# Batch 0's transposes one pair ahead, half of its queries and keys by casting DMA, and a new load order on GpSimd

## The chip, the cores and the metric

The kernel runs on one core of a Trainium2 chip. The metric is the device time of one execution in microseconds (us); each version was run several times, and medians are quoted with their range. The profile shown of a version is of one execution under the hardware profiler, for every version but the kernel before one of those counted; its span is some 1.7 us shorter than the time of the same execution. All runs quoted here are of the fast state.

Names: PE is the matrix engine, DVE VectorE, ACT ScalarE, POOL GpSimd, SP the engine that only issues transfers.

## The reference

```python
# q, k, v: (B=8, H=8, S=576, D=64); beacon_k, beacon_v: 16 more keys and values per head, never masked
k_all = concat([beacon_k, k], axis=2); v_all = concat([beacon_v, v], axis=2)
scores = q @ k_all.T / sqrt(D)           # causal mask over the 576 ordinary keys
a = softmax(scores)
x = (a @ v_all)                          # (B*S, H*D) = (4608, 512)
h = max(x @ w1, x @ w2, x @ w3)          # d_ff = 768
out = h @ w_out                          # (4608, 512) float32
```

## The kernel before: the parts that matter

The kernel goes through 32 head pairs, four to a batch. A pair's queries and keys are turned on PE by 28 transposes, copied out of PSUM by DVE, and give scores in six steps; ACT takes the exponentials. Every second pair, the value products of a finished quad of heads are put between the score steps. From batch 1 on, the feed-forward units of the batch before fill PE's gaps. Batch 0 has no such filler. Its first ten feed-forward units come in a block behind batch 0's last value products, and batch 1 starts behind them.

```python
def emit_transposes(p):                       # pair p of batch b
    ...
    if b == 0:                                # batch 0 arrives in float32 and is cast on the engines
        q32, k32 = stage.pop(pi)
        nc.vector.tensor_copy(q_sb[:, pair_heads(pi), :], q32)
        nc.scalar.copy(k_sb[:, pair_heads(pi), :], k32)
    q_ps = turn(qs, QP, QR)                   # 12 transposes on PE
    k_ps = turn(ks, KP, KR)                   # 16 transposes on PE
    for e in range(2):
        nc.vector.tensor_copy(qz[p % NQZ][e][hs], q_ps[hs])
    nc.vector.tensor_copy(kT, k_ps.rearrange("d r p -> d p r"))
...
def emit_all():
    load_qk_first(0); load_qk_first(1)        # float32, queues of SP and ACT
    for t in range(n_kt): build_mask(t)       # POOL
    for t in range(n_kt): load_v(0, t)        # casting DMA, POOL's queue, as all below
    load_w_in(0, d_ff // 2); load_w_in(d_ff // 2, d_ff)
    load_w_out()
    load_qk(1, slice(0, H))
    for t in range(n_kt): load_v(1, t)
    emit_transposes(0)
    for p in range(NPAIR):
        for c in range(len(chunks)):          # six score steps
            emit_scores(p, c)                 # 2 matmuls, 2 exponentials, masks
            if p != PPB and p >= 2 and p % 2 == 0 and 1 <= c <= 3:
                emit_pv(p // 2 - 1, c - 1)    # value products
            if c == 3 and p + 1 < NPAIR and p + 1 != PPB:
                if b == 0 and pi < 2: load_qk_first(pi + 2)
                emit_transposes(p + 1)
            ...
        if p == PPB - 1:                      # end of batch 0
            ... # last value products, ten feed-forward units
            emit_transposes(p + 1)            # first pair of batch 1
```

The softmax here doesn't subtract the row's maximum and nothing guards it: scores larger than these inputs give would overflow.

## Time and profile before

| | before |
|---|---|
| median of 3 runs | 345.58 us (345.57 to 346.87) |
| profiled span | 343.9 us |
| PE busy, whole span | 91% |
| first exponential of batch 0 | 9.75 us |
| first feed-forward matmul | 41.54 us |
| from there to the end | 302.3 us |

The prediction shows the views that matter: the slices of the span, the instructions in order of time, and the stages of batch 0. In the timeline the first two numbers are start and length in us, and the bracket is how long the engine had stood idle and what ended it. In a stage line the numbers behind the stretch and its length are busy us and instruction counts of PE, PE's weight loads, DVE, ACT and POOL, then the granted clock of PE, the share of the DMA engines (the times of all packets over those of 16 engines, so it can pass 1) and GB/s.

I call the time up to the first feed-forward matmul the ramp, and the rest the stretch. In the stretch PE is nearly full.

### The profile page before, as it was taken

How to read it: one execution, taken by the hardware profiler on the slowest of the kernel's cores; microseconds unless marked ns; L12 is line 12 of the kernel's file. 1: busy time of each engine (PE TensorE's matmuls, PEld its weight loads, DVE VectorE, ACT ScalarE, POOL GpSimd, SP SyncE). 2: the span in 40 equal slices, each digit the busy share in tenths (PEclk: the TensorE clock that was granted, in tenths of full speed). 3: DMA queues.
4: the chain of work that ended last, by engine and by line, in shares of the span. 5: the costliest groups of instructions: out<-in, count | busy, mean ns of one | idle time of the engine just before them, and what ended most of it. 6: DMA issues, size and time to landing. Idle time of an engine off the chain costs nothing.

```text
span 343.9 us, 9797 instructions
## 1 busy us (share of the span) xinstructions
PE 311.6 (91%) x4011; PEld 174.4 (51%) x4064; DVE 185.8 (54%) x338; ACT 187.0 (54%) x507; POOL 162.0 (47%) x441
## 2 busy tenths in 40 slices
PE   1676897989999999999999999999999999999993
PEld 1344543545565556565655555555555555444441
DVE  4445354456565655655565556565555564545552
ACT  2675626875666557665757475647573765120210
POOL 6778105982666367636753575457542433000000
PEclk9998799999999999999999999999999999999999
DMA  8999950991993189306940694059713100402204
GB/s 171 194 188 158 184 38 2 154 60 32 173 108 27 32 137 145 27 22 117 173 26 4 132 172 34 2 105 181 46 8 93 34 2 3 122 2 52 70 2 123
DMA packets 62165, 28.85 MB, mean 84 GB/s; under 512 B 42792, under 2 KB 56920, under 8 KB 62120
## 3 DMA queue, kind: packets, MB, share of 16 engines
q0 software_dynamic: 54880, 16.38, 45.6%
q1 hardware_dynamic: 6928, 11.24, 12.0%
q8 instruction: 32, 0.52, 0.6%
q10 hardware_dynamic: 312, 0.59, 0.6%
q14 instruction: 13, 0.11, 0.1%
HBM read 35.13 MB, written 9.44 MB: 130 GB/s over the span
## 4 chain that ended last, share of the span: by engine, by line
PE 73%; DVE 9%; DMA 8%; POOL 5%; issue 3%; ACT 1%; DVEq 0%
PE fps L332 32%; PE fps L349 12%; PE sc L247 10%; PE pv L293 10%; PE sc L332 5%; DMA k_sb<-in_k_dram 4%; PE sc L208 3%; DVE kT L226 2%; DVE hT L342 2%; DMA v_sb<-in_v_dram 2%; DMA w_sb<-in_moe_w_dram 2%; PE sc L349 2%; POOL w_sb L171 2%; DVE xT L310 1%; POOL at_sb L271 1%
## 5 line engine op out<-in xcount | busy, mean ns | idle before, releaser
L255 ACT ACTIVATE at_sb<-sc 128x288 bf16<-128x288 f32 (+4 forms) x384 | 129.0, 406 | 77.4 <-PE sc L247 74.7
L271 POOL TENSOR_SCALAR_AFFINE_SELECT at_sb<-at_sb 128x57 bf16<-128x57 bf16 (+1 forms) x336 | 93.5, 300 | 113.1 <-ACT at_sb L255 109.0
L332 PE MATMUL fps<-xT,w_sb 128*128 128x512 bf16 x540 | 141.4, 379 | 4.8 <-issue 2.7
L342 DVE TENSOR_TENSOR hT<-hT,fps 128x512 bf16<-128x512 bf16 x96 | 65.8, 686 | 66.0 <-PE fps L332 55.7
L332 PEld LDWEIGHTS <-w_sb 128*128 128x128 bf16 x648 | 59.6, 98 | 58.7 <-issue 3.6
L247 PEld LDWEIGHTS <-kT 128*128 128x128 bf16 (+1 forms) x384 | 38.6, 106 | 46.7 <-DVE kT L226 6.5
L340 ACT CAST hT<-fps 128x512 bf16<-128x512 f32 x48 | 28.2, 587 | 42.8 <-PE fps L332 37.7
L349 PE MATMUL fps<-w_out_sb,hT 128*128 128x512 bf16 x171 | 42.7, 380 | 1.6 <-issue 1.3
L310 DVE TENSOR_TENSOR xT<-pv,recip 128x288 bf16<-128x288 f32 x64 | 27.7, 454 | 29.6 <-ACT recip L305 22.4
L161 POOL DMA_DIRECT2D v_sb<-in_v_dram x40 | 34.0, 860 | 6.1 <-DMA w_out_sb<-in_moe_w_out_dram 3.7
L293 PE MATMUL pv<-at_sb,v_sb 128*32 128x288 bf16 (+4 forms) x1280 | 33.1, 242 | 0.2 <-ACT lnd L303 0.2
L357 DVE COPY y<-fps 128x512 f32<-128x512 f32 x31 | 21.4, 690 | 20.8 <-PE fps L349 16.4
L247 PE MATMUL sc<-qz_107,kT 128*128 128x288 bf16 (+2 forms) x96 | 28.4, 300 | 4.5 <-DVE kT L226 3.6
L293 PEld LDWEIGHTS <-v_sb 128*32 128x32 bf16 (+1 forms) x1280 | 25.8, 98 | 12.6 <-issue 11.3
L247 PE MATMUL sc<-qz_111,kT 128*128 128x288 bf16 (+2 forms) x96 | 28.8, 301 | 2.2 <-DVE kT L226 1.8
L349 PEld LDWEIGHTS <-hT 128*128 128x128 bf16 x216 | 19.5, 98 | 20.0 <-DVE hT L342 0.4
L247 PE MATMUL sc<-qz_113,kT 128*128 128x288 bf16 (+2 forms) x96 | 28.7, 301 | 0.3
L247 PE MATMUL sc<-qz_109,kT 128*128 128x288 bf16 (+2 forms) x96 | 28.4, 302 | 0.2 <-DVE kT L226 0.2
L226 DVE COPY kT<-sc 128x592 bf16<-128x592 bf16 x28 | 21.7, 775 | 0.9
L208 PEld LDWEIGHTS <-q_sb 96*64 96x64 bf16 x384 | 10.7, 114 | 18.9 <-DVE q_sb L219 13.2
L293 PE MATMUL pv<-at_sb,ones 128*32 128x288 bf16 (+4 forms) x640 | 18.7, 246 | 0.6 <-DVE xT L310 0.6
L332 PE MATMUL sc<-xT,w_sb 128*128 128x512 bf16 x71 | 18.4, 379 | 0.1
(50 smaller groups left out, 190.0 us busy)
## 6 DMA issues: line engine op xcount, KB each, us to landing
out_dram<-y SPq DMA_DIRECT2D x24, 192.0 KB, 2.2
q_sb<-in_q_dram POOLq DMA_DIRECT2D x7, 576.0 KB, 7.4
k_sb<-in_k_dram POOLq DMA_DIRECT2D x7, 576.0 KB, 11.2
v_sb<-in_v_dram POOLq DMA_DIRECT2D x24, 128.0 KB, 4.7
out_dram<-y SPq DMA_DIRECT2D x24, 128.0 KB, 2.2
w_sb<-in_moe_w_dram POOLq DMA_DIRECT2D x24, 96.0 KB, 5.5
out_dram<-y SPq DMA_DIRECT2D x24, 64.0 KB, 1.6
v_sb<-in_v_dram POOLq DMA_DIRECT2D x8, 112.0 KB, 4.5
```

What stands on the lines that cost most here:

```text
L161: nc.gpsimd.dma_start(out=v_sb[lo : lo + n, t], in_=v[b, :, t0 : t0 + n, :].rearrange("h p d -> p h d"),)
L226: nc.vector.tensor_copy(kT, k_ps.rearrange("d r p -> d p r"))
L247: nc.tensor.matmul(ps[0:n, 0 : nr * w].rearrange("k (r p) -> k r p", p=w), kT[:, 128 * t : 128 * t + n], qz[p % NQZ][e][:, r0:r1, p0:QP], ...
L255: nc.scalar.activation(out=at_sb[0:n, t, j0 + e, r0:r1, p0:QP], in_=sc[e][0:n, 0 : nr * w].rearrange("k (r p) -> k r p", p=w), func=AF.Exp ...
L271: nc.gpsimd.affine_select(out=view, in_=view, compare_op=ALU.is_ge, fill=0.0, base=QR * p0 + r0 - k_tok[t], pattern=[[1, nr], [QR, p1 - p0 ...
L293: nc.tensor.matmul(ps[32 * j : 32 * j + 32, :, p0:QP], lhsT, at_sb[0:n, t, j, rs, p0:QP], start=(t == 0), stop=(t == n_kt - 1), tile_posit ...
L310: nc.vector.tensor_mul(xs.rearrange("c (r p) -> c r p", p=QP), ps, state["recip", hf])
L332: nc.tensor.matmul(ps, w_in[i][:, ct, 128 * ft : 128 * (ft + 1)], xT[:, ct, t0 : t0 + TOKB], start=(ct == 0), stop=(ct == n_ct - 1),)
L340: nc.scalar.copy(hT[:, ft, :], ps)
L342: nc.vector.tensor_max(hT[:, ft, :], hT[:, ft, :], ps)
L349: nc.tensor.matmul(ps, hT[:, ft, 128 * tt : 128 * (tt + 1)], w_out_sb[:, ft, :], start=(ft == 0), stop=(ft == n_ft - 1),)
L357: nc.vector.tensor_copy(y, ps)
```

## The change

Three things are meant to shorten the ramp. The next pair's transposes are issued behind the pair's first score step, and no longer behind its fourth, so that their copies are ready when the pair ends. Pairs 2 and 3 of batch 0 come in bfloat16 by casting DMA, so that ACT and DVE need not cast them. On POOL's queue pair 2 comes first of all, masks are built between value loads, and batch 1's queries and keys go ahead of the output weight.

```diff
-        if b == 0:                                   # in emit_transposes
-            q32, k32 = stage.pop(pi)
-            nc.vector.tensor_copy(q_sb[:, pair_heads(pi), :], q32)
-            nc.scalar.copy(k_sb[:, pair_heads(pi), :], k32)
+    def cast_first(pi):                              # now its own function, for pairs 0 and 1
+        ...
         load_qk_first(0)
         load_qk_first(1)
-        for t in range(n_kt):
-            build_mask(t)
+        load_qk(0, pair_heads(2))
+        make_identity(nc, ident)                     # was at the head of the kernel
         for t in range(n_kt):
             load_v(0, t)
+            if t == 2:
+                for u in range(n_kt):
+                    build_mask(u)
+        load_qk(0, pair_heads(3))
         load_w_in(0, d_ff // 2)
         load_w_in(d_ff // 2, d_ff)
+        load_qk(1, slice(0, H))
         load_w_out()
-        load_qk(1, slice(0, H))
...
+        cast_first(0)
         emit_transposes(0)
+        cast_first(1)
...
-                emit_scores(p, c)
+                if p < PPB - 1 and c == 0:
+                    emit_scores(p, c, lambda: emit_transposes(p + 1))   # between exponentials and masks
+                else:
+                    emit_scores(p, c)
...
-                if c == 3 and p + 1 < NPAIR and p + 1 != PPB:
-                    if b == 0 and pi < 2:
-                        load_qk_first(pi + 2)
+                if c == 3 and b > 0 and p + 1 < NPAIR:
                     emit_transposes(p + 1)
```

## The prediction

> **The bound.** I first read the page's busy shares: the matrix engine (PE) is busy for 91% of the 343.9 us. The 40 slices show where the other 9% is: from the ninth slice on PE stands at 8 or 9 tenths, but the first five read 1, 6, 7, 6, 8. The ramp, batch 0's attention, is not PE bound, and the change touches only that.
>
> ```profile
> PE   1676897989999999999999999999999999999993
> DMA  8999950991993189306940694059713100402204
> ```
>
> Each digit is 8.6 us. DMA is at 8 or 9 for the first five slices, then alternates: the start is also when everything is loaded.
>
> Next the instructions in order of time (start, length, engine, line, work, idle before), from the middle of head pair 0 to the first scores of pair 1:
>
> ```profile
> 12.08 0.30 DVE L267 TENSOR_TENSOR at_sb<-at_sb,mask 128x264 bf16<-128x264 bf16 x1 [0.75 <-ACT at_sb L255]
> 12.47 1.08 ACT L220 CAST k_sb<-k_125 74x1024 bf16<-74x1024 f32 x1
> 12.76 0.30 DVE L267 TENSOR_TENSOR at_sb<-at_sb,mask 128x264 bf16<-128x264 bf16 x1 [0.39 <-ACT at_sb L255]
> 12.98 0.55 DVE L219 CAST q_sb<-q_124 96x768 bf16<-96x768 f32 x1
> ...
> 13.58 0.69 PE L208 MATMUL fps<-ident,q_sb 96*64 96x96 bf16 x12 [1.81 <-DVE q_sb L219]
> ...
> 14.07 0.70 PE L208 MATMUL fps<-ident,k_sb 74*64 74x74 bf16 x16
> ...
> 15.29 0.78 DVE L226 COPY kT<-fps 128x592 bf16<-128x592 bf16 x1
> ...
> 16.12 0.42 PE L247 MATMUL sc<-qz_111,kT 128*128 128x288 bf16 x1 [0.75 <-DVE kT L226]
> ```
>
> It is one chain across three engines: masks, cast, transposes, two qz copies (14.31 to 15.25), kT copy, scores. ScalarE (ACT), which must do all the exponentials, stands still in it. The stages, cut at the first exponential of each pair, say it in busy time (columns: stretch, length, PE, PE loads, DVE, ACT, POOL, granted clock, DMA share, GB/s):
>
> ```profile
> 9.75:16.58 6.83, 4.27 (x42) 2.57 (x41) 3.55 (x10) 4.63 (x14) 4.31 (x9) 1.00 1.57 188
> 16.58:23.34 6.76, 4.27 (x42) 2.57 (x41) 3.56 (x10) 4.62 (x14) 4.84 (x10) 1.00 1.18 203
> 23.34:33.90 10.56, 7.81 (x162) 4.80 (x160) 5.11 (x14) 6.46 (x17) 9.94 (x15) 0.91 1.13 159
> 33.90:37.48 3.58, 3.38 (x23) 1.67 (x24) 1.20 (x5) 3.58 (x12) 0.46 (x1) 0.50 1.26 193
> 37.48:41.54 4.06, 3.18 (x117) 2.67 (x111) 1.37 (x5) 1.71 (x5) 1.15 (x2) 0.84 1.53 187
> ```
>
> Pairs 0, 1 and 2 fill no engine: 6.8 us for 4.6 of ACT. Only pair 3 (no cast, no transposes) is ACT bound, 3.58 of 3.58. Then the last value products, and at 41.54 us the first feed-forward matmul: from there PE is nearly full, about 34.0 of every 35 us. So the end moves with that instant, and that is what I predict.
>
> **The Trainium skill.** "TensorE: Matmul & The Clock Gate", section "Part 1: The HAM clock gate", says that PE starts at half clock and moves between half and full after windows of 3413 ns, by how busy it was. The trace agrees; the granted clock changes on such edges (same columns):
>
> ```profile
> 25.14:28.55 3.41, 3.41 (x60) 1.65 (x52) 1.12 (x3) 2.13 (x6) 3.41 (x7) 1.00 1.21 174
> 28.55:31.97 3.42, 1.74 (x71) 1.52 (x71) 1.82 (x5) 1.95 (x4) 3.42 (x5) 1.00 1.03 141
> 31.97:35.38 3.41, 2.34 (x11) 1.29 (x10) 2.06 (x7) 2.30 (x9) 1.31 (x2) 0.50 1.17 167
> 35.38:38.79 3.41, 3.21 (x54) 1.96 (x56) 1.14 (x5) 2.76 (x10) 0.88 (x1) 0.50 1.30 198
> ```
>
> After a full window (3.41) the matmuls run at double pace at 28.55; after one with 1.74 us busy the clock is 0.50; after one with 3.21 it is back. The column reads 1.00 before the first change too, but there PE is at half pace: a 288 wide score starts every 0.24 us at 16 us and every 0.13 us at 53 us. A window with 2.67 of 3.42 us (14.9 to 18.3) had not raised it. So nearly all of batch 0 runs at half pace.
>
> "DMA: Bandwidth & Descriptors", section "SWDGE vs HWDGE vs iDMA", says that only GpSimd's queue (POOL) can cast, with descriptors written by software; its section "Queues, rings and completion order" says that each of the 16 engines takes turns between the rings that have work. The trace agrees with the first (all bf16 loads are on POOL) and shows the sharing: from 2 to 7 us the two hardware queues alone moved the 1.19 MB of pairs 0 and 1 at some 240 GB/s; when POOL's loads joined at 7 the rate fell to 147.
>
> **The change, part by part.** The order of instructions on each engine, before against after, shows that only the start moves.
>
> *Pairs 2 and 3 by casting DMA.* Removed: two key casts on ACT, 1.08 and 1.04 us, and two query casts on DVE, 0.55 each. All four stood in the chain. Pair 2's load is POOL's first instruction, at about 0.8 us in place of values at 4.7; its three issues take some 0.6 us each, and it should land by about 8. Pair 3 comes behind the values. These are 4,736 small packets; before, POOL's queue reached 915 packets in one microsecond when alone, so 5.3 us from about 7.5, then pair 3's 0.59 MB (fp32) in 2 us: about 15. It is wanted at 20.5, below. No stall.
>
> *The price at the start.* Pair 0's inputs landed at 5.9 (queries) and 6.6 (keys). Now a third ring shares the engines with them. 1.78 MB in place of 1.19 through engines that later reached some 330 GB/s of source bytes (16 to 18 us: 0.37 MB plain, 0.15 MB cast, which is 0.30 at source): I choose keys 0.7 us later. From keys to first exponential took 9.75 - 6.6 = 3.15 us, unchanged, so the first exponential comes at 10.45. Pair 1's casts now stand in ACT's and DVE's wait for pair 0 and cost little.
>
> *Transposes one pair ahead, after the first score step.* Removed from each of three pair changes: the wait for transposes (0.5 + 0.7), qz copies (0.9) and kT copy (0.78), less what is put into the pair. Put in: PE does 28 transposes, 1.25 us at half pace, between score steps 0 and 1. The score buffers (4) let ACT have only step 0 in hand, two exponentials, 0.66 us; then it waits for the transposes plus one 0.24 us matmul and its latency. I take a gap of 1.15 us a pair. ACT's exponentials are 2.91 + 0.83 = 3.74 us a pair. Adding, and leaving 0.2 and 0.3 us for handovers:
>
> - pair 0: 3.74 + 1.15 + 0.2 = 5.1, was 6.83
> - pair 1: 3.74 + 1.15 + 0.3 = 5.2, was 6.76
> - pair 2: PE bound. Its own PE work at half pace is 2.8 (scores) + 1.25 (transposes) + 6 value passes x 0.71 = 8.3; PE is full here, so one window edge falls inside and the passes after it take 0.41; I take 7.5, was 10.56
> - pair 3: ACT bound, 3.6, as before
> - last value products: before, 4.06 with their first half at half pace. The chain pass, logarithm 0.41, exponential 0.44, two products 0.41 each, pass, and again stays; I take 3.6
>
> Sum: 10.45 + 5.1 + 5.2 + 7.5 + 3.6 + 3.6 = 35.45, against 41.54: 6.1 us earlier. Against this, pair 3 keeps PE only some 40% busy at full pace (1.4 of 3.6 us), so the clock may fall just before the feed-forward starts: a half-speed window costs 1.7 us; I give it 0.35 and subtract 0.6. The matmul at 41.54 is also followed by a stall of 0.44 us, of which I give back 0.3. Net gain 5.8 us.
>
> *Load order.* Batch 1's queries and keys move ahead of the output weight. They landed at 39.6 and 43.4 us (issue plus time to landing) and batch 1's transposes ran at 50.67, so the earlier batch 1 wants them at about 45. As the output weight took 6.3 us of queue (30.4 to 36.7) they now land near 37: hidden. The first half of the input weights landed by 24 (issued by 18.4, 5.5 to landing), wanted at 35. Masks move behind three value loads on POOL and are built by about 8 us, wanted at 11. Identity is ready by 3.5, wanted at 7.
>
> **Rivals.** (a) *Loads become the bound.* DMA is saturated to about 46 us; if pair 3 lands after 21 us, PE, which runs in order, stands at its transposes in the middle of pair 2, and 3 us are given back. Against it: 5 us of slack. Or the third ring delays pair 0 by 2 to 3 us and that much is lost; for it, the drop to 147 GB/s; against it, that the early rings hold few bytes. Either would give about 342. (b) *The clock.* The denser pairs put PE at about 4.1 of 5.2 us, 79%, close to the 78% window that did not raise the clock. If it rises in pair 0 or 1, the gap shrinks from 1.15 to about 0.3 and pair 2 becomes ACT bound (3.74 + 1.7 = 5.5 us): 2 to 3 us more, 337. (c) *The gain is hidden downstream.* Batch 1 could wait for DMA or for POOL, which builds its masks after its loads. Against it: POOL stood idle 13.1 us before its first mask of batch 1, at 53.8 us, and now frees near 37. I hold this unlikely; 344 if so.
>
> **Range and chances.** 345.58 - 5.8 = 339.8 us. The free terms (start 0 to +2, pair gaps, window phase twice 1.7) give about 2.1 us of spread, so 337.0 to 342.5. Two per cent is 6.9 us, half a spread beyond my middle: 0.30 faster, 0.68 within, 0.02 slower, since no part adds work.
>
> **What would show it.** First exponential near 10.5 us; exponentials of the next pair following within 0.3 us and a gap near 1 us after step 0; no casts from pair 2 on; ACT over 70% busy in pairs 0 and 1; pair 3's transposes not waiting on a load; first feed-forward matmul near 35.5; the stretch from there to the end unchanged near 302 us. I am wrong if the PE waits for loads in pairs 2 or 3, if the feed-forward starts at half pace for more than one window, or if the later stretch grows.

## The result

| | before | after |
|---|---|---|
| median | 345.94 us (345.57 to 346.87, 4 runs) | 336.48 us (335.23 to 337.03, 4 runs) |
| ratio, 95% interval | | 0.9718 (0.9683 to 0.9753) |
| profiled span | 343.9 us | 335.0 us |
| first feed-forward matmul | 41.54 us | 32.24 us |
| from there to the end | 302.3 us | 302.8 us |

The ratio is the mean time of one kernel's fast runs over that of the other's in the same rounds, so it isn't quite the ratio of the medians. The change gains 9.5 us where 5.8 were predicted; 336.48 lies 0.5 us below the predicted range. A later control of the same file, on the chip time of other experiments, gave 337.86 us (335.93 to 338.16, 5 runs), ratio 0.9762: inside the range, still well below its middle. Why one kernel gives two such medians is a part of the answer.

The page after, PE and DMA in 40 slices of the span; the first five of PE now read 1, 9, 9, 8, 9:

```profile
PE   1998979899999999999999999999999999999994
DMA  7999968906940596229941993179404000402204
```

The timeline after, from pair 1's key cast to the first exponentials of pair 2 with transposes behind it:

```profile
9.06 1.04 ACT L153 CAST k_sb<-k_121 74x1024 bf16<-74x1024 f32 x1 [2.20 <-DMA k_121<-in_beacon_k_dram]
...
10.01 0.70 ACT L255 ACTIVATE at_sb<-sc 128x288 bf16<-128x288 f32 x2
...
11.25 3.77 ACT L255 ACTIVATE at_sb<-sc 128x288 bf16<-128x288 f32 x12 [0.54 <-PE sc L247]
...
14.44 0.69 PE L212 MATMUL fps<-ident,q_sb 96*64 96x96 bf16 x12
...
16.01 3.65 ACT L255 ACTIVATE at_sb<-sc 128x288 bf16<-128x288 f32 x12 [0.99 <-PE sc L247]
...
19.08 0.45 PE L212 MATMUL fps<-ident,q_sb 96*64 96x96 bf16 x12
...
20.06 0.71 ACT L255 ACTIVATE at_sb<-sc 128x288 bf16<-128x288 f32 x2 [0.40 <-PE sc L247]
```

ACT runs from pair 0 into pair 1's first step without a stop (12 exponentials in one piece) and waits only behind that step, while PE transposes: 0.54, 0.99 and 0.40 us. The same 12 transposes take 0.69 us at 14.4 and 0.45 at 19.1: PE's clock rose between them.

The stages after, cut as those of before, at the first exponential of each pair, the end of the exponentials and the first feed-forward matmul:

```profile
10.01:14.30 4.29, 4.08 (x30) 2.09 (x28) 2.77 (x8) 3.73 (x13) 4.29 (x8) 1.00 1.80 149
14.30:18.95 4.65, 4.46 (x41) 2.52 (x40) 2.97 (x10) 3.65 (x13) 4.49 (x9) 1.00 1.21 173
18.95:25.09 6.14, 5.59 (x161) 3.95 (x161) 4.20 (x13) 5.34 (x17) 5.70 (x12) 1.00 1.19 168
25.09:28.68 3.59, 2.98 (x25) 1.24 (x25) 1.83 (x8) 3.59 (x13) 2.64 (x5) 1.00 1.16 161
28.68:32.24 3.56, 2.65 (x108) 2.19 (x105) 1.13 (x5) 1.71 (x5) 3.56 (x6) 1.00 1.11 137
```

The three long pairs fell from 6.83, 6.76 and 10.56 us to 4.29, 4.65 and 6.14. In pairs 0 and 1 PE is now busy for 95% of the time (4.08 of 4.29, 4.46 of 4.65), where it was 63%. Pair 3 was and is bound by ACT.

### The profile page after: what moved, and what is told of

Its sections match the earlier page's. It is cut to its first block, busy times and chain, and to the rows that moved or that the text cites. A ratio compares the mean times of both kernels' runs of the same rounds, so it can differ in the third digit from the quotient of the medians.

```text
span 335.0 us, 9841 instructions
## 1 busy us (share of the span) xinstructions
PE 315.7 (94%) x4064; PEld 172.9 (52%) x4064; DVE 184.9 (55%) x336; ACT 185.0 (55%) x505; POOL 166.4 (50%) x447
## 4 chain that ended last, share of the span: by engine, by line
PE 81%; DVE 9%; ACT 5%; DMA 2%; issue 2%; SPq 0%; DVEq 0%; ACTq 0%
PE fps L334 34%; PE fps L351 12%; PE sc L247 12%; PE pv L295 11%; PE sc L334 5%; ACT at_sb L255 4%; PE sc L212 4%; DVE kT L226 3%; DVE hT L344 2%; DMA k_121<-in_beacon_k_dram 2%; PE sc L351 2%; DVE xT L312 2%; DVE qz_109 L225 1%; PE fps L212 1%; DVE qz_105 L225 1%
## 5 line engine op out<-in xcount | busy, mean ns | idle before, releaser
L334 PE MATMUL fps<-xT,w_sb 128*128 128x512 bf16 x576 | 147.4, 381 | 0.9
L247 PEld LDWEIGHTS <-kT 128*128 128x128 bf16 (+1 forms) x384 | 37.7, 103 | 46.3 <-issue 7.4
L342 ACT CAST hT<-fps 128x512 bf16<-128x512 f32 x48 | 28.2, 587 | 42.8 <-PE fps L334 37.7
L351 PE MATMUL fps<-w_out_sb,hT 128*128 128x512 bf16 x186 | 44.8, 380 | 0.0
L295 PE MATMUL pv<-at_sb,v_sb 128*32 128x288 bf16 (+4 forms) x1280 | 32.2, 236 | 0.5 <-DVE xT L312 0.2
L247 PE MATMUL sc<-qz_103,kT 128*128 128x288 bf16 (+2 forms) x96 | 27.7, 294 | 4.0 <-DVE kT L226 3.1
L295 PEld LDWEIGHTS <-v_sb 128*32 128x32 bf16 (+1 forms) x1280 | 25.3, 96 | 11.8 <-issue 10.8
L247 PE MATMUL sc<-qz_107,kT 128*128 128x288 bf16 (+2 forms) x96 | 27.8, 291 | 1.2 <-ACT at_sb L255 0.8
L247 PE MATMUL sc<-qz_109,kT 128*128 128x288 bf16 (+2 forms) x96 | 27.8, 290 | 0.6 <-ACT at_sb L255 0.2
L247 PE MATMUL sc<-qz_105,kT 128*128 128x288 bf16 (+2 forms) x96 | 27.6, 293 | 0.1
L295 PE MATMUL pv<-at_sb,ones 128*32 128x288 bf16 (+4 forms) x640 | 17.6, 237 | 0.8 <-DVE xT L312 0.4
L212 PEld LDWEIGHTS <-q_sb 96*64 96x64 bf16 x384 | 10.9, 115 | 13.2 <-DVE q_sb L152 6.7
```

Source lines behind the costliest of these rows:

```text
L212: nc.tensor.transpose(ps[64 * e : 64 * e + 64, r, :], src[e][:, r * D : (r + 1) * D], ident[0:n, 0:n],)
L247: nc.tensor.matmul(ps[0:n, 0 : nr * w].rearrange("k (r p) -> k r p", p=w), kT[:, 128 * t : 128 * t + n], qz[p % NQZ][e][:, r0:r1, p0:QP], ...
L295: nc.tensor.matmul(ps[32 * j : 32 * j + 32, :, p0:QP], lhsT, at_sb[0:n, t, j, rs, p0:QP], start=(t == 0), stop=(t == n_kt - 1), tile_posit ...
L334: nc.tensor.matmul(ps, w_in[i][:, ct, 128 * ft : 128 * (ft + 1)], xT[:, ct, t0 : t0 + TOKB], start=(ct == 0), stop=(ct == n_ct - 1),)
L342: nc.scalar.copy(hT[:, ft, :], ps)
L351: nc.tensor.matmul(ps, hT[:, ft, 128 * tt : 128 * (tt + 1)], w_out_sb[:, ft, :], start=(ft == 0), stop=(ft == n_ft - 1),)
```

## The experiments

Theory S: the order of instructions, together with the casts that left ACT and DVE, closed the chain across the engines, and the early clock of PE follows from that. Theory L: the casting loads and their place in the queue did most. Theory C: PE's clock, being up earlier, is a large part on its own. Theory W: batch 1's keys must come sooner once batch 0 is short.

| run | what it is | median, us (range) | ratio to before | profiled run, us | first exponential | clock rises | first feed-forward |
|---|---|---|---|---|---|---|---|
| before | | 345.58 to 346.09 (by call) | 1 | 345.67 | 9.75 | 28.5, down 31.9 to 38.8 | 41.54 |
| only_order | order alone | 340.72 (338.95 to 341.81) | 0.9845 | 338.95 | 9.97 | 18.9 | 33.64 |
| order_qk | order, batch 1's keys early | 339.42 (338.17 to 340.38) | 0.9814 | 339.97 | 9.98 | 13.2, down 20.0 to 23.5 | 34.05 |
| cast_only | casting loads alone | 341.67 (341.03 to 342.81) | 0.9887 | 341.53 | 9.51 | 19.9, down 30.2 to 33.6 | 37.07 |
| only_loads | casting loads and all load order | 341.90 (341.58 to 342.21) | 0.9882 | 342.11 | 10.67 | 24.9, down 31.7 to 38.5 | 38.57 |
| before_warm | before, PE kept busy | 344.09 (342.72 to 345.84) | 0.9945 | 344.30 | 10.19 | 10.8 | 40.21 |
| after | the changed kernel | 336.48 (335.23 to 337.03) | 0.9718 | 336.69 | 10.01 | 17.9 | 32.24 |
| after_again | the same, control | 337.86 (335.93 to 338.16) | 0.9762 | 338.10 | 10.35 | 22.6 | 34.13 |
| after_warm | after, PE busy from the start | 338.05 (336.96 to 339.05) | 0.9773 | 336.96 | 10.60 | 4.3, down 7.7 to 11.1 | 32.09 |
| after_step1 | transposes behind step 1 | 336.51 (335.79 to 337.83) | 0.9729 | 337.83 | 10.56 | 22.3 | 33.83 |
| masks_first | masks ahead of the loads | 336.07 (335.00 to 338.20) | 0.9724 | 335.17 | 10.24 | 13.2 | 31.98 |
| wout_first | output weight first again | 337.31 (336.25 to 338.87) | 0.9748 | 337.88 | 10.12 | 19.1, down 29.3 to 32.7 | 33.16 |
| combined | step 1, masks first, batch 1 early | 335.01 (334.01 to 335.22) | 0.9678 | 334.01 | 9.73 | 16.7 | 31.78 |
| early_only | batch 1's first transposes early | 334.27 (333.43 to 335.18) | 0.9671 | 335.18 | 9.75 | 21.6 | 33.38 |

The last four columns are of the one profiled execution of each, which can lie at either end of a version's runs (only_order's is its fastest, early_only's its slowest); the clock changes are those within the ramp that the trace records. The stage times of one profile and the medians need not agree to the last half microsecond, since, as will be seen, executions of one kernel differ in the clock. All these kernels gave correct results.

### only_order: the order alone

```diff
 # the kernel before, with cast_first() and between= as in the change
+        cast_first(0)
+        load_qk_first(2)
         emit_transposes(0)
+        cast_first(1)
+        load_qk_first(3)
...
+                if p < PPB - 1 and c == 0: emit_scores(p, c, lambda: emit_transposes(p + 1))
+                if c == 4 and p + 2 < PPB: cast_first(p + 2)
```

> The kernel before, with the transposes one pair ahead and the casts one pair ahead of them, but all four pairs still loaded in float32 and cast on the engines, and every load in its old order. Theory S (the order of instructions gave most of the 9.5 us, by closing the gaps of ScalarE, and the denser PE raised the clock early as a consequence): each of pairs 0 and 1 costs the 1.05 us of a key cast more than in the changed kernel, so the first feed-forward matmul near 34.3 us and about 338.5 us in all. Rival L (the casting loads and the load order gave most): 343 us or more, first feed-forward matmul after 38.5.

It gave 340.72 us, between the two theories. The profile is of its fastest run, 338.95 us, close to theory S's 338.5; it has the first feed-forward matmul at 33.64, a little earlier than theory S put it, and then takes 303.6 us to the end, where the kernel before takes 302.3. The waits of PE at the start of batch 1, in this kernel:

```profile
42.77 0.45 PE L214 MATMUL sc<-ident,q_sb 96*64 96x96 bf16 x12
44.32 0.46 PE L214 MATMUL sc<-ident,k_sb 74*64 74x74 bf16 x16 [1.10 <-DMA k_sb<-in_beacon_k_dram]
45.65 2.29 PE L249 MATMUL sc<-qz,kT 128*128 128x288 bf16 x8 [0.87 <-DVE kT L228]
```

The queries are turned at 42.8, the keys 1.10 us late, for their load is still under way. With the load order of before, a shorter batch 0 runs into batch 1's loads. Order alone is the largest single part, 5.4 us, and loses some of its gain here.

### order_qk: the same with batch 1's queries and keys ahead of the output weight

```diff
-        load_w_out()
         load_qk(1, slice(0, H))
+        load_w_out()
```

> The kernel only_order with batch 1's queries and keys ahead of the output weight. Theory W (only_order, 340.7 us, fell short of its 338.5 because PE waited 1.10 us for batch 1's keys and its clock fell in that wait): the wait goes, 338 to 339 us. Rival: the casts on ScalarE and VectorE are the whole difference to the changed kernel: 340.5 us, no change.

It gave 339.42 us. The intervals of the two ratios (0.9808 to 0.9883 and 0.9788 to 0.9840) overlap, so 1.3 us of gain is likely and not proved by the times. The wait is gone in the profile: the key transposes run at 43.46 with no wait, right behind the queries. That is worth 0.6 us and not 1.10, since PE then waits longer for the key copies, 1.56 us in place of 0.87: from batch 1's first transposes to its first scores it takes 2.88 us in only_order (42.77 to 45.65) and 2.28 here (43.18 to 45.46). The run was 0.4 us longer than theory W allowed; its clock had fallen twice.

### only_loads and cast_only: the loads without the order

only_loads is the changed kernel with the transposes put back behind step 3. It keeps the early cast of pair 1, which in cast_only stands in the change from pair 0 to pair 1.

```diff
-                if p < PPB - 1 and c == 0:
-                    emit_scores(p, c, lambda: emit_transposes(p + 1))
-                else:
-                    emit_scores(p, c)
+                emit_scores(p, c)
```

> The changed kernel with the transposes put back behind step 3 of the pair before: casting loads and load order kept. Theory S: the three pair changes lose their casts, about 1.05 us each, and keep transposes, copies and the wait, so about 342.5 us, first feed-forward matmul near 38.5, clock still at half until pair 2. Rival L: about 338 us.

It gave 341.90 us with the first feed-forward matmul at 38.57, as theory S had it (342.5 and 38.5); the clock rose at 24.9, in pair 2.

cast_only is the kernel before with nothing but the casting loads for pairs 2 and 3, put behind the values.

```diff
-        if b == 0:
+        if b == 0 and pi < 2:                        # only pairs 0 and 1 are cast on the engines
...
             load_v(0, t)
+        load_qk(0, pair_heads(2))
+        load_qk(0, pair_heads(3))
```

> The kernel before with pairs 2 and 3 loaded by casting DMA behind the values, and nothing moved. Theory S: two of the three pair changes lose their cast, 1.05 us each, so 2 us: 343.7 us. Rival L (the loads matter by being first or by using the engines less): within 0.5 us of only_loads, 341.9; or slower than before, if pair 2's load comes after the 20.3 us at which it is wanted.

It gave 341.67 us, twice the gain that I expected and the same as only_loads. That is rival L's number; but its first reason, loads that stand first, cannot be the cause here, where they stand behind the values. Its second, that the loads use the DMA engines less, is not separated from theory S by a run. Nor do the two runs price the place in the queue cleanly: in only_loads pair 0 is shorter by its cast (5.43 us against 6.97) and the first exponential later (10.67 against 9.51). masks_first, below, tests the place alone. What the loads took off ACT and DVE is in the timeline of ACT: pair 0's change, which still has its cast, is as before (first exponentials at 9.51 and 16.48, 6.97 us), pair 1's is 5.29 us (to 21.77), 1.5 us less than in the kernel before, and pair 2's is 7.92 (to 29.69), 2.6 less.

```profile
9.51 2.91 ACT L255 ACTIVATE at_sb<-sc 128x288 bf16<-128x288 f32 x8 [2.09 <-PE sc L247]
12.23 1.08 ACT L220 CAST k_sb<-k 74x1024 bf16<-74x1024 f32 x1
15.00 0.83 ACT L255 ACTIVATE at_sb<-sc 128x210 bf16<-128x210 f32 x4 [1.69 <-PE sc L247]
16.48 2.91 ACT L255 ACTIVATE at_sb<-sc 128x288 bf16<-128x288 f32 x8 [0.66 <-PE sc L247]
```

Pair 1's gain is the cast, 1.05 us, and the query cast that stood behind a mask on DVE. Pair 2's is the cast and the clock, which had risen at 19.9 in place of 28.5, so that the value passes ran at full pace.

### before_warm and after_warm: the clock by itself

Dummy matmuls, whose results are never read, fill PE's waits. In the kernel before they stand ahead of and behind every pair's transposes in batch 0; in the changed kernel only at the start.

```diff
+    warm_src = const.tile([128, 448], BF16, name="warm_src")     # ones
+    def warm_up(n):
+        ps = pv_psum.tile([128, 512], FP32, name="pv")
+        for _ in range(n):
+            nc.tensor.matmul(ps[:, 0:448], warm_src[:, 0:128], warm_src, start=True, stop=True)
...
+        warm_up(12)
         emit_transposes(0)
+        warm_up(4)
# before_warm also: warm_up(8) ahead of the transposes of pairs 1 to 3, warm_up(4) behind them
```

> The kernel before with dummy matmuls in all of PE's waits of batch 0, so that its clock is at full pace from about 7 us. If the earlier clock alone was a large part of the gain (rival C): 341 to 342 us. If the chain across engines is what matters (theory S): PE's part of the chain shrinks by 0.6 us in three pair changes and pair 2's value passes by 2 us at most, of which the chain returns part: 343.5 to 344.5 us.

The clock was up from 10.8 us on and never fell in the ramp, and the gain is 2.0 us (ratio 0.9945, 0.9931 to 0.9958). So the clock alone, without the shorter chain, is a small part: theory C falls for the kernel before. The number may be too low for the clock's worth there, since in pair 2 the dummies themselves waited for a PSUM buffer and held the transposes up, by some 0.45 us (from the end of the query cast at 29.75 to 30.20).

> The changed kernel with 12 dummy matmuls of 448 columns on PE before the first transposes, while it waits for the first load, and 4 behind them. Theory C (the clock of PE still costs in batch 0): full pace from some 7 us on, the gap after step 0 falls from 0.99 to about 0.3 us in pair 1 and pair 0 shortens likewise; 1 us less, 335.4 us. Rival (ScalarE and the loads bound the ramp whatever the clock): 336.5 us, same.

It gave 338.05 us, not faster, and the first feed-forward matmul at 32.09 in the profile, which is of its fastest run (336.96 us). The clock rose at 4.3 and fell again at 7.7, behind a window in which PE, with 16 dummies, was still busy for only 1.58 of 3.41 us, as it waited for loads and copies; it was up for good from 11.1. The gaps behind step 0 were 0.33, 0.40 and 0.40 us, as theory C had said. In this run the gain was lost at the front: pair 1's keys landed at 9.64 and the first exponential came at 10.60. That may be chance, for without dummies these keys landed anywhere from 8.77 to 9.72. Two of its four runs took 339.0 us, at a mean granted clock of 0.986 to 0.987 where the profiled run has 0.990; where they lost it, no kept trace shows. From first exponential to first feed-forward matmul it took 21.49 us, in the changed kernel 22.23.

### after_step1, masks_first: where the transposes and the masks stand

```diff
-                if p < PPB - 1 and c == 0:                  # after_step1
+                if p < PPB - 1 and c == 1:
```

> The changed kernel with the next pair's transposes behind score step 1 in place of step 0, so that ScalarE has four exponentials in hand while PE transposes. Theory G (the gaps of 0.54, 0.99 and 0.40 us behind step 0 are the price of where the transposes stand): the gaps nearly go, first feed-forward matmul near 30.9, about 335.2 us. Rival: PE bounds the pairs while its clock is at half, the gap only moves behind step 1: 336.5 us.

It gave 336.51 us, no gain that the medians show. The gap moved behind step 1, as the rival said: ACT, in order of time,

```profile
10.56 5.17 ACT L255 ACTIVATE at_sb<-sc 128x288 bf16<-128x288 f32 x16
16.75 3.74 ACT L255 ACTIVATE at_sb<-sc 128x468 bf16<-128x468 f32 x12 [1.02 <-PE sc L247]
```

has no gap in pair 0 and one of 1.02 us in pair 1. In pair 1 PE has 4.5 us of work at half pace and ACT 3.7, so PE binds and ACT's wait can be moved and not removed. In pair 0 something may be left: the ramp from the first exponential took 23.27 us here and 23.78 in after_again, whose clock rose about as late.

```diff
-        load_qk(0, pair_heads(2))                           # masks_first
         make_identity(nc, ident)
+        for t in range(n_kt):
+            build_mask(t)
+        load_qk(0, pair_heads(2))
         for t in range(n_kt):
             load_v(0, t)
-            if t == 2:
-                for u in range(n_kt):
-                    build_mask(u)
```

> The changed kernel with identity and masks ahead of all loads on GpSimd, as in the kernel before, so that pair 2's casting load starts at about 4.7 us in place of 1.4. Theory D (the early casting load takes engine time from pair 1's keys, which landed at 9.06 in the changed kernel, and pair 1's cast stands ahead of pair 0's first exponential): pair 1's keys near 7.5, first exponential near 9.2 in place of 10.0, 0.8 us faster, about 335.7 us. Rival F (loads first is a gain): pair 3's load, 3 us later, is waited for; 337.5 us or more.

It gave 336.07 us: same, and both theories are wrong. Pair 1's keys didn't land earlier for POOL's queue being empty:

```profile
9.29 1.04 ACT L153 CAST k_sb<-k 74x1024 bf16<-74x1024 f32 x1 [1.64 <-DMA k<-in_beacon_k_dram]
```

9.29 us, against 9.06 and 9.40 in the two profiles of the changed kernel. By the profile, what is waited for is the 8 KB load of pair 1's beacon keys, which SP issues last, at 2.0 us, behind 288 KB of queries. And pair 3's load was not late. The first exponential and the ramp are those of the changed kernel with an early clock.

### wout_first: batch 1's keys

```diff
-        load_qk(1, slice(0, H))
         load_w_out()
+        load_qk(1, slice(0, H))
```

> The changed kernel with the output weight back ahead of batch 1's queries and keys. Theory W (once batch 0 is short, batch 1's inputs are wanted at 41.6 us, and the old order lands them at some 43 to 44): its transposes wait 2 us for keys, the clock falls in that wait, 338.5 to 340 us. My prediction's own claim (hidden): 336.5 us.

It gave 337.31 us, ratio 0.9748 (0.9723 to 0.9774), which is within the scatter of the changed kernel's two results. The profile shows the wait that theory W named, at less than half its size:

```profile
43.32 0.46 PE L212 MATMUL sc<-ident,k_sb 74*64 74x74 bf16 x16 [0.77 <-DMA k_sb<-in_beacon_k_dram]
```

The wait for the key copies behind it is shorter in return, 0.87 us in place of 1.56. From batch 1's first transposes to its first scores it takes 2.55 us here (42.10 to 44.65) and 2.28 in the changed kernel (41.60 to 43.88), so by these traces the new order is worth about 0.3 us there. In the changed kernel the keys landed at 38.9 us (issue at 28.52 plus 10.4 to landing for their last piece) and were wanted at 41.6: hidden, as predicted, with 2.7 us to spare.

### after_again: the control

> The changed kernel, unedited, as a control on the same chip as the three others. 336 to 337 us; the runs with the lower mean clock are the longer ones, as each half-pace window costs up to 1.7 us.

The unedited kernel gave 337.86 us, above what I expected, and the mean granted clock did not order its runs: it was 0.995 in all five, whose times go from 335.93 to 338.16 us. The two profiles of this kernel, of runs of 336.69 and 338.10 us, show where 1.4 us lie between two executions. The stages again, same cuts:

```profile
10.35:14.65 4.30, 4.02 (x28) 2.09 (x28) 2.79 (x8) 3.73 (x14) 4.30 (x8) 1.00 1.61 129
14.65:19.41 4.76, 4.63 (x41) 2.56 (x40) 3.08 (x10) 3.74 (x13) 3.98 (x8) 1.00 1.17 163
19.41:26.75 7.34, 6.75 (x161) 4.73 (x161) 4.25 (x13) 5.53 (x16) 7.10 (x15) 1.00 1.18 164
26.75:30.35 3.60, 3.00 (x25) 1.24 (x25) 1.68 (x8) 3.60 (x13) 3.08 (x5) 1.00 1.12 162
30.35:34.13 3.78, 2.72 (x108) 2.31 (x107) 1.34 (x5) 1.71 (x4) 3.06 (x4) 1.00 1.23 170
```

Pair 2 takes 7.34 us here and 6.14 there. The instructions are the same; here the clock rose at 22.6, in the middle of pair 2's value passes, there at 17.9, before they began. The busy time of PE in the clock's windows ahead of each rise, first the changed kernel's profile, then the control's:

```profile
11.11:14.52 3.41, 3.28 (x14) 1.38 (x14) 2.06 (x7) 3.25 (x11) 3.41 (x7) 1.00 1.74 160
14.52:17.93 3.41, 3.41 (x36) 2.13 (x37) 2.30 (x7) 2.42 (x8) 3.30 (x7) 1.00 1.22 171
```

```profile
15.77:19.18 3.41, 3.28 (x19) 1.57 (x14) 2.29 (x7) 2.83 (x10) 2.92 (x6) 1.00 1.16 159
19.18:22.59 3.41, 3.41 (x70) 2.27 (x70) 2.42 (x7) 2.03 (x7) 3.41 (x7) 1.00 1.15 156
```

In these two profiles the window that PE filled (3.41) ended with the clock up, and those with 3.28 us busy did not raise it. That is no rule: wout_first, with the same PE and ACT code in the ramp, got its clock behind this window:

```profile
15.66:19.07 3.41, 3.28 (x16) 1.53 (x12) 2.27 (x8) 2.96 (x10) 2.91 (x6) 1.00 1.18 168
```

The Trainium skill, "TensorE: Matmul & The Clock Gate", "Part 1: The HAM clock gate", says that the window is free-running and "doesn't reset when your kernel starts". The traces agree: of the profiles whose ramp has the same PE and ACT code, the clock rose at 13.2 (masks_first), 17.9 (after), 21.6 (early_only) and 22.6 us (after_again), and from the first exponential to the first feed-forward matmul they took 21.74, 22.23, 23.63 and 23.78 us. The order is the same. (wout_first, 19.1 and 23.04, has the clock down again for the last value products.) So an early clock goes with a short ramp, by 1.55 us between two executions of the changed kernel and by 2.0 over the four kernels. That the phase of the window, where its edges fall in the ramp, decides when the clock rises fits this, but is not shown: the first edge behind the first exponential comes 2.00 us after it in after_again and 2.12 in wout_first, nearly the same, and yet the clock rose one window earlier in wout_first.

### early_only and combined: a faster version

```diff
                 while done[0] < allowed:
+                    if done[0] == 8:
+                        emit_transposes(p + 1)
                     emit_ffn(ready, allowed)
-                emit_transposes(p + 1)
# combined: this, masks_first and after_step1 together
```

> The changed kernel with batch 1's first transposes between feed-forward units 8 and 9 and nothing else. If this alone makes the combined kernel faster than the changed one: 335.0 us, and the 1.56 us wait of PE for the key copies is gone. Rival (the wait only moves to batch 1's keys or to the exponentials): 336.3 us.

> Transposes behind step 1, masks first, and batch 1's first transposes between feed-forward units 8 and 9, so that the 1.56 us in which PE waited for the copies of its keys lie beside two units. If all three hold: 1.3 + 0.8 + 1.6 us less than the changed kernel, 332.8 us. If batch 1's keys, which landed at 38.9, are late for transposes at about 37.5: the wait only moves, about 335 us.

early_only gave 334.27 us (ratio 0.9671, 0.9650 to 0.9692), faster than the changed kernel of the same call (0.9762, 0.9737 to 0.9787). In the changed kernel PE stood idle at the start of batch 1, as it did in the kernel before (1.56 us at 52.95):

```profile
43.88 0.30 PE L247 MATMUL sc<-qz_103,kT 128*128 128x288 bf16 x1 [1.56 <-DVE kT L226]
```

In early_only two feed-forward units lie beside the copies and the scores follow with no wait:

```profile
40.92 0.44 PE L212 MATMUL sc<-ident,k_sb 74*64 74x74 bf16 x16
41.30 1.90 PE L334 MATMUL fps<-xT,w_sb 128*128 128x512 bf16 x7
43.21 0.66 PE L247 MATMUL sc<-qz,kT 128*128 128x288 bf16 x4
```

There is a second effect: in its profile the clock never falls in the stretch, until the very end, while in both profiles of the changed kernel it went to half for one window at the start of batch 1 (45.2 to 48.6 us in the first), behind a window with 1.72 of 3.41 us busy. Each run's mean granted clock says the same: all five runs of early_only have 0.998 or more, while of the nine of the changed kernel seven have 0.995 and two 1.000. combined gave 335.01 us, not better than early_only: its other two parts added nothing, as their own runs had shown. That is the number of its second expectation, but the wait for batch 1's keys was only 0.17 us there.

## Why the prediction was wrong

**What held.** The ramp was the place, and the end moved with the first feed-forward matmul: the stretch is 302.3 us before and 302.8 and 302.2 us in the two profiles after. PE did not wait for the loads of pairs 2 or 3. Batch 1's loads stayed hidden, with 2.7 us of slack where I had put some 8. The gap behind step 0 exists. Pair 3 at 3.6 us and the last value products at 3.6 are right (3.59 and 3.56).

**What failed.** The place and the mechanism, a chain shortened by order and casts, were right. What failed are sizes in the sum: the gap and handover of pairs 0 and 1, and pair 2 at half clock. The terms, with what the two profiles measured:

| term | predicted | after | after_again |
|---|---|---|---|
| first exponential | 10.45 | 10.01 | 10.35 |
| pair 0 | 5.1 | 4.29 | 4.30 |
| pair 1 | 5.2 | 4.65 | 4.76 |
| pair 2 | 7.5 | 6.14 | 7.34 |
| pair 3 | 3.6 | 3.59 | 3.60 |
| last value products | 3.6 | 3.56 | 3.78 |
| sum, first feed-forward matmul | 35.45 | 32.24 | 34.13 |

1. "I take a gap of 1.15 us a pair", and "leaving 0.2 and 0.3 us for handovers". The gaps were 0.54 (pair 0) and 0.99, and there was no handover: ACT went from one pair into the next without a stop. This is the lasting part of the miss, 1.2 to 1.4 us over pairs 0 and 1 in both profiles. In pair 0 the gap was half of what I took because pair 1's key cast had held ACT's first exponentials back to 10.01, by when PE was far into the transposes. In effect I had charged for PE's work twice, as a gap and as a handover.

2. "pair 2: PE bound [...] I take 7.5". This rests on the clock at half until an edge inside pair 2. In after_again that was so, and the term is right to 0.2 us. In the first profile the clock rose before pair 2 and it took 6.14. My rival (b) named this, with 337 us, and 336.48 came; but it gave it for a PE "at about 4.1 of 5.2 us, 79%", where PE was 95% busy, and had ACT bind pair 2, where ACT was busy for 5.34 and PE for 5.59 of the 6.14 us. Whether a run gets the early clock is luck as far as these runs show. With it the miss of the whole sum is 3.2 us, without it 1.3.

3. "I choose keys 0.7 us later": for pair 0's keys there is no such price. Pair 0's key cast started at 5.81 and 6.21 us in the changed kernel, 6.61 before, and anywhere from 5.8 to 6.6 in the other kernels, with POOL's loads early or late; masks_first, with POOL's loads late, had 6.60. The rates that the price rested on were read loosely: before the change it was 229 GB/s from 2 to 7 us, and 147 to 249 in the five microseconds behind, not a fall to 147. The first exponential came nearly when I said, for another reason: the cast of pair 1, which waited for its load until 9.06, stands ahead of it in ACT's order. I had written that it would "cost little". By the trace, pair 0's scores were issued at 8.70, so it held the first exponentials back by some 0.85 us, as estimated from the 0.46 us that lay between the same two in the kernel before (9.29 to 9.75). This alone does not lengthen the ramp, for pair 0's second step stands behind pair 1's transposes on PE, and these wait for the same cast. What starts the ramp is therefore the landing of pair 1's keys: in all seven profiles with the transposes behind step 0 and PE at half pace there, the cast began at 8.80 to 9.40 us and the second step's exponentials 2.19 or 2.20 us later. What an earlier landing would be worth, no run tests.

4. "subtract 0.6" for a clock that falls just before the feed-forward block. It did not fall there in the two profiles, though it did in wout_first (29.3 to 32.7); it fell later, at the start of batch 1, and the stretch shows no net cost against before. The 0.3 us given back for a stall of 0.44 us behind the matmul at 41.54 had no ground either: the next ones start at 41.80 and 42.16, then every 0.21 to 0.22 us. And "pairs 0, 1 and 2 fill no engine: 6.8 us for 4.6 of ACT" holds for pairs 0 and 1; pair 2 took 10.56 us, with POOL busy for 9.94.

So the middle of 339.8 was too slow by the first and fourth points in both profiles and by the second in the one with the early clock, and the range was too narrow on its fast side by half a microsecond.

**Where the gain comes from.** Order alone gives 5.4 us, or about 6.3 with batch 1's keys early (345.76 less 339.42); casting loads alone give 4.1. Together they give 7.9 to 9.5, so the two nearly add up, with an overlap of 1.0 to 2.5 us. The early clock is part of both: in every profile with a shorter chain it rose earlier, at 13.2 to 24.9 us without dummies, than in the one profile of the kernel before (28.5), but not in the order of how busy PE was (19.9 in cast_only, 22.6 in after_again). Alone the clock is worth about 2 us in the kernel before. That loads stand first in the queue is worth nothing that these runs can see (masks_first).

**What stays open.** What decides when the clock rises, and how much of the scatter between executions comes from it: each run's mean granted clock is on record, but it reads 1.00 before the first change, so it tells falls and not the rise. Why only_order and order_qk, with ramps as short as after_again's, end later (0.9 and 1.9 us by the profiled runs, 2.9 and 1.6 by the medians) is explained only in part: 0.6 us of waiting in the one, a clock that fell twice in the other.

## What to carry to other kernels

When a chain of casts, transposes and copies stands between two pieces of work, issue it one piece ahead and take each link off an engine that has to do the main work; order and links were each worth four to six microseconds here, and the time of the loads in the queue nothing that could be seen. Before you price PE's share at half pace, ask how dense PE will be after the change, and give the range the width of an early and a late clock. After a ramp has been shortened, look again at what follows it: here the next batch's loads were wanted 9 us earlier (41.6 against 50.7), and filling the wait for the copies at its start, which had always been there, was worth another 2.1 to 2.7 us of stretch in the profiles (300.1 us in early_only), 3.6 us by the medians of one call.

## What the Trainium skill lacked or had wrong

- "TensorE: Matmul & The Clock Gate" gives no busy share at which the clock rises or falls, and PE's busy time in these profiles, which is modelled, yields none. Up to the start of batch 1, at half pace, every window with 3.40 or 3.41 us busy raised it; windows with 3.21 (before) and 3.28 (wout_first) did too, while others with 3.28 (after, after_again) did not. At full pace windows with 1.72, 1.74 and 2.63 (wout_first, ahead of 29.3) lowered it, and one with 1.85 (masks_first, ahead of 43.9) did not.
- The same page calls the warm-up less than 1% of a typical span. Between the two profiles of the changed kernel the ramp differs by 1.55 us of 336, with the clock up at 17.9 and at 22.6, which agrees; but that is more than a quarter of the gain of 5.8 us that was predicted.
- No page says that the granted clock of a profile can read 1.00 up to the first recorded change although PE runs at half pace: here 12 transposes took 0.69 us at 14.4 us and 0.45 at 19.1, both under 1.00.
- "DMA: Bandwidth & Descriptors" gives some 0.6 us to the first byte for transfers of SP and ACT, and no figure for one that stands behind others. Here an 8 KB load, issued by SP at 2.0 us behind 288 KB on the same queue, was waited for, by the profiles, until 8.77 to 9.72 us in the eleven that wait for it; the page's account of rings that are consumed in order agrees with that.
